# Long convolution and gated feed-forward on one core: some units of the third step taken out by ScalarE and GpSimd, and the first group's matrices made inside that step

## The chip, the cores and the metric

The kernel runs on one core of a Trainium2 chip. The metric is the device time of one execution in microseconds; the time of a kernel is the median over its runs. The engines are called PE (TensorE; its weight loads PEld), DVE (VectorE), ACT (ScalarE), POOL (GpSimd) and SP (SyncE, which here issues every DMA). Each takes its instructions in the order in which the program lists them.

## The reference

A batch of 4 sequences of 12480 positions and 128 channels goes through a gated convolution over the whole sequence, with a filter that a small network makes from position embeddings. The result goes, as 49920 rows, through a feed-forward layer of width 2048 whose gate is a cosine.

```
h_filt = (relu(pos_emb @ w1) @ w2) * exp(-0.01 * pos)[:, None]
Uf = rfft(x * v, n=2*S, axis=1);  Hf = rfft(h_filt, n=2*S, axis=0)
y  = irfft(Uf * Hf, n=2*S, axis=1)[:, :S, :]
t  = (x * y).reshape(B * S, D)
h  = t @ w_in
out = (h * cos(h)) @ w_out
```

Everything is float32; `w_in` and `w_out` come as 64-bit floats and are converted on the chip.

## The kernel before

The Fourier transforms are matrix products. A length is split as 96 x 120 (`N1`, `N2`), and a batch goes through four steps, all on one large buffer `slots` (128 partitions, 64 pairs of channels, 240 columns, 2): `f1` (units of one pair of channels, line 407 and its evictions), `f2` (units of two frequencies, a product with the filter's transform, lines 448 to 474), `i1` (the third step, 64 units of one pair of channels, lines 479 to 490) and `i2` (30 groups of four matrices each, lines 504 to 511), after which rows are ready for the feed-forward layer. Batch 0's first three steps stand alone at the start of the program; its `i2`, and all steps of the other three batches, are woven into the feed-forward layer's steps (lines 743 to 768), which fill PE for the rest of the time.

The order of work is written out by hand. Every piece of work is a Python generator, and what it emits between two yields lands in the engines' lists at that place. `units` runs the matmuls of unit j beside the evictions of unit j-1, and with `before(j)` prepares what unit j needs. `beside` runs one such generator, counts its yields i, and in between takes a step of `convert_units` (when i is a multiple of 14) or of a second generator (when i is a multiple of 5).

The third step of batch 0, in the stretch from about 270 to 337 us, is the call `beside(i1_units(bank), ..., some_groups)` at line 907. In it three kinds of work are mixed:

- `i1_units`: for each of 64 units PE makes four products into one of eight PSUM banks (the trace counts eight passes for them); ACT copies half of the bank to the tile `other` (line 487, two buffers); DVE takes the sum and the difference of the other half of the bank and `other` into `slots` (line 489, two instructions of 96 x 240).
- `convert_units`: eight pieces of `w_out`. For each, DVE takes exponent and mantissa (L133, L141), GpSimd makes the power (L135, L137), ACT converts two halves (L144, L146), GpSimd adds them (L147); one step later DVE joins the sign (L151) and GpSimd multiplies (L156). `raw` has three buffers, `low` one.
- `some_groups`: groups 2, 7, 12, 17, 22 and 27 of the matrices that `i2` needs. A matrix is two ACT instructions (L291, L296, the latter into `spare`, two buffers) and a GpSimd sum (L297); after four of them the group is stored to `td`. At its end, `next(backs[0])` makes group 0 in one go for the coming `i2` (tile `tm`: its first matrix with a GpSimd sum, the three others with L293 on DVE), and loads `xs`.

The tables `rows` and `tw_t` that the matrices are made from are loaded at line 899, once the second step's buffers are free. The second step's units end with two GpSimd sums each (L474), which write what `i1` reads. The first matmul of `i2` (L504) needs all of `slots` and group 0's matrices.

Of the kernel before, what the change touches and what calls it, by code (L numbers as in the profile page):

```python
# [9 lines left out]
F32 = mybir.dt.float32  # L10
# [20 lines left out]
def kernel(  # L31
# [46 lines left out]
    nc = tc.nc  # L78
# [4 lines left out]
    N1, N2 = 96, 120  # L83
# [16 lines left out]
    G = BANK // D  # L100
# [49 lines left out]
    def float32_join(dst, raw, power, high):  # L150
# [6 lines left out]
        if dst.space == DRAM:  # L157
# [5 lines left out]
                 for c in range(0, DFF, WCOL)]  # L163
    out_pieces = [(slice(c, c + WCOL // D), out_words[:, c:c + WCOL // D, :, :])
                  for c in range(0, NFC, WCOL // D)]
# [133 lines left out]
    def make_w(w, k1, **how):  # L299


        turn(w, even[:, 0, :], even[:, 1, :], tw_w[:, 0, k1:k1 + 1], tw_w[:, 1, k1:k1 + 1],
             **how)
# [149 lines left out]
            for r, src in enumerate((ftile[0:KE, :, k, :], above[0:KE, :, k - KF, :])):  # L453
                nc.tensor.matmul(pi[:, r], w[:, i, :], src, start=True, stop=True)

    def f2_product(pool, ps, h, k1, whole):


        y = parts[0:N2, :, k1:k1 + 2, :, :].rearrange("p r k b i -> p r b (k i)")
        t = pool.tile([N2, 2, CB, 4], F32, name="t", bufs=1 + whole)  # L460
        uu = ps[0:N2, :].rearrange("p (r b j) -> p r b j", r=2, j=4)
        if whole:
            for r, (dst, hh) in enumerate(((y, h[:, :, :, :]), (t[:, :, :, :], h[:, ::-1, :, :]))):
                u = uu[:, r]
                twice = bass.AP(tensor=u.tensor, offset=u.offset,
                                ap=[u.ap[0], [0, 2], *u.ap[1:]])
                nc.vector.tensor_tensor(dst, twice, hh, op=ALU.mult)  # L467
                yield
        for r, op in ((0, ALU.subtract), (1, ALU.add)):
            if not whole:  # L470
                nc.vector.tensor_tensor(y[:, r], uu[:, 0], h[:, r], op=ALU.mult)
                yield
                nc.vector.tensor_tensor(t[:, r], uu[:, 1], h[:, 1 - r], op=ALU.mult)
            nc.gpsimd.tensor_tensor(y[:, r], y[:, r], t[:, r], op=op)  # L474
            yield

    def i1_mm(ps, b, i):
# [3 lines left out]
                parts[0:N2, r, :, b, i],  # L481
                cs[:, r, :], start=True, stop=True)

    def i1_evict(pool, ps, b):
        pj = ps[0:N1, 0:4 * N2].rearrange("p (i r j) -> p r j i", i=2, r=2)
        other = pool.tile([N1, N2, 2], F32, name="other")
        nc.scalar.copy(out=other[:, :, :], in_=pj[:, 1])  # L487
        for h, op in ((0, ALU.add), (1, ALU.subtract)):
            nc.vector.tensor_tensor(slots[0:N1, b, h * N2:(h + 1) * N2, :], pj[:, 0],  # L489
                                    other[:, :, :], op=op)  # L490
            yield

    def i2_mm(ps, t, g, part):
# [36 lines left out]
    def units(n, steps, before, mm, after, parts, ahead=2, skip=0):  # L530


        for j in range(min(ahead, n)):
            for _ in before(j) or ():
                pass
        yield 0.0
        last = iter(())
        for j in range(n):
            early = iter(before(j + ahead) or () if j + ahead < n else ())
            now = None  # L540
            for i in range(parts):
                if i == skip or 2 * (i - skip) == max(parts, 2):
                    now = mm(j, now, int(i > skip))
                if i == 0 and parts == 1:
                    now = mm(j, now, 1)
                next(last, None)
                next(early, None)
                yield steps / parts
            for _ in early:
                pass  # L550
            next(last, None)
            last = after(j, now)
        for _ in last:
            pass
        yield REST

    SOME = range(2, NG, 5)
# [52 lines left out]
    def f2_both_units(bank):  # L610

        with tc.tile_pool(name="both", bufs=2) as pool:
            ws = {}

            def before(j):
                ws[j] = pool.tile([KE, 2, N2], F32, name="w")
                for i in range(2):
                    make_w(ws[j][:, i, :], 2 * j + i, half=bank)
                nc.sync.dma_start(wd[j, :, :, :], ws[j][:, :, :])

            def mm(j, ps, i):
                if i == 0:
                    ps = bank(), bank()
                for filt in range(2):
                    f2_mm(ps[filt], ws[j], 2 * j, i, filt=filt == 1)
                return ps

            def after(j, ps):
                h = pool.tile([N2, 2, CB, 4], F32, name="h", bufs=3)
                nc.scalar.activation(h[:, :, :, :].rearrange("p r b j -> p (r b j)"),  # L630
                                     ps[1][0:N2, :], AF.Copy, scale=1.0 / M)
                nc.sync.dma_start(hd[j, :, :, :, :], h[:, :, :, :])
                yield from f2_product(pool, ps[0], h, 2 * j, True)

            yield from units(N1 // 2, F2_STEPS, before, mm, after, 4, ahead=1)

    def i1_units(bank):
        with tc.tile_pool(name="mid", bufs=2) as pool:
            def mm(j, ps, i):
                if i == 0:  # L640
                    ps = bank()
                i1_mm(ps, j, i)
                return ps

            yield from units(CB, I1_STEPS, lambda j: None, mm,
                             lambda j, ps: i1_evict(pool, ps, j), 2)

    def make_group(pool, g, t, summed):

# [8 lines left out]

    def some_groups(pool):
        for g in SOME:  # L660
            t = pool.tile([N1, G, 2, R], F32, name="some", bufs=2)
            yield from make_group(pool, g, t, G)
        next(backs[0])

    def i2_units(bank, b, bufs):

        with tc.tile_pool(name="back", bufs=2, side="left" if b else "right") as pool:
            ts, xss = {}, {}

            def before(j):  # L670
                ts[j] = pool.tile([N1, G, 2, R], F32, name="tm", bufs=bufs)
                xss[j] = pool.tile([R, 2, UA * D], F32, name="xs", bufs=bufs)
                load_pairs(xss[j], x, b, n2s(j)[0], n2s(j)[UA])
                if b == 0 and j not in SOME:
                    return make_group(pool, j, ts[j], 1)
                nc.sync.dma_start(ts[j][:, :, :, :], td[j, :, :, :, :])

            def mm(j, ps, i):
                if i == 0:
                    ps = bank()  # L680
                i2_mm(ps, ts[j], j, i)
                return ps

            yield from units(NG, I2_STEPS, before, mm,
                             lambda j, ps: i2_out(pool, ps, xss.pop(j), b, j),
                             4 if b == 0 else 2, ahead=bufs - 1, skip=int(b == 0))

    def inverse_units(bank, b):

        if b + 1 == B:
            yield from i2_units(bank, b, 3)
            return
        new = u_units(b + 1, 3, slots[0:R, :, :, :],
                      lambda j, half: nc.gpsimd if b == 0 and j % 2 > half else nc.vector,
                      side="right" if b else "left")
        parts = 4 if b == 0 else 2
        for i, steps in enumerate(i2_units(bank, b, 2)):
            if i > 2 * parts:  # L700
                for _ in range(i % parts > 0 if b == 0 else 1 + i % 2):
                    next(new, None)
            yield steps * (FIRST_STEPS if b == 0 else I2U_STEPS) / I2_STEPS
        yield from new
# [95 lines left out]
    with tc.manual_schedule():  # L800
        with tc.tile_pool(name="psum", bufs=8, space=PSUM) as psum, \
                ExitStack() as first:
            def bank():
                return psum.tile([P, BANK], F32, name="ps")

            spool = ctx.enter_context(tc.tile_pool(name="slots", bufs=1))
            slots = spool.tile([P, CB, 2 * N2, 2], F32, name="slots")
# [64 lines left out]


            backs = [inverse_units(lambda: bank(), b) for b in range(B)]

            def beside(units, pieces, more=lambda pool: iter(())):
                with tc.tile_pool(name="convert", bufs=1) as pool:
                    convert, other = convert_units(pool, pieces), more(pool)
                    for i, _ in enumerate(units):
                        if i % 14 == 0:  # L880
                            next(convert, None)
                        elif i % 5 == 0:
                            next(other, None)
                    for _ in [*convert, *other]:
                        pass
# [17 lines left out]
            w_out_sb = wpool.tile([P, NFC, D], F32, name="w_out_sb")  # L903
            quarter = wpool.tile([P, 1], F32, name="quarter")
            nc.vector.memset(quarter[:, :], 0.25)
            nc.sync.dma_start(w_in_sb[:, :], wind[:, :])
            beside(i1_units(bank), [(w_out_sb[:, c, :], w) for c, w in out_pieces], some_groups)

        ps_acc = ctx.enter_context(tc.tile_pool(name="ps_acc", bufs=1, space=PSUM))
        ps_h = ctx.enter_context(tc.tile_pool(name="ps_h", bufs=4, space=PSUM))  # L910
# [36 lines left out]
        steps = [(n, c) for n in range(NALL) for c in range(NFC)]  # L947
        hidden, gates, ots, obs = {}, {}, {}, {}
        for i in range(len(steps) + LAG):
            if i < len(steps):  # L950
                n, c = steps[i]
# [53 lines left out]
```

## Time and profile before

| | |
|---|---|
| median of four runs | 3759.27 us |
| lowest and highest run | 3757.18, 3764.23 us |
| the profiled execution | 3757.18 us, span 3755.4 us |
| PE, DVE, ACT, POOL busy over the span | 98%, 74%, 67%, 68% |
| granted PE clock, mean | 0.996 |
| second step of batch 0 | about 168 to 271 us |
| third step of batch 0 | 271.07 (first i1 pass) to 336.62 (first i2 pass) |

The page's first part gives the busy time of each engine, the windows view the same for a stretch of time. A timeline shows one instruction, or a run of like ones (`x8`), per line: start, length, engine, line of the program, operation, result and operands with their shapes, and in brackets how long the engine had stood idle and which instruction let it go. A length is that of the instruction, not the distance to the next start, which is shorter on DVE and ACT, where successive instructions overlap.

### The profile page before, as it was taken

What the parts mean: (1) busy time and instruction counts of PE and PEld (TensorE: products, weight loads), DVE (VectorE), ACT (ScalarE), POOL (GpSimd) and SP (SyncE); (2) the same over time, 40 slices, a digit from 0 to 9 for tenths busy, and PEclk for the clock granted to TensorE, in tenths of its full rate; (3) what the DMA queues carried; (4) which work ended last, traced back from release to release, by engine and by line L of the source; (5) the groups of instructions that cost most, each with busy time, mean ns of one, the idle gap of its engine ahead of it and who ended that gap; (6) DMA issues with size and microseconds to landing.
All of it is one profiled execution on the core that took longest, in us unless ns stands there. A gap on an engine that the chain in (4) does not pass through costs nothing.

```text
span 3755.4 us, 47177 instructions
## 1 busy us (share of the span) xinstructions
PE 3687.4 (98%) x13546; PEld 2106.4 (56%) x13546; DVE 2772.9 (74%) x5586; ACT 2508.3 (67%) x4660; POOL 2558.6 (68%) x2318
## 2 busy tenths in 40 slices
PE   7898999999999999999999999999999999999999
PEld 6777555555566556555565556555566544444444
DVE  8887997777866787788767776788765566666666
ACT  5756777766655557766655567666664677777777
POOL 7666775588845665688745664788644677777776
PEclk9999999999999999999999999999999999999999
DMA  6263551022203550122104530122105200000000
GB/s 167 66 184 109 155 165 36 24 76 75 72 13 94 178 151 12 42 78 79 50 18 130 181 102 21 52 80 76 37 21 175 73 23 17 17 23 18 17 23 13
DMA packets 209499, 276.14 MB, mean 74 GB/s; under 512 B 17111, under 2 KB 146535, under 8 KB 209111
## 3 DMA queue, kind: packets, MB, share of 16 engines
q1 hardware_dynamic: 209239, 273.12, 24.3%
q8 instruction: 109, 1.79, 0.2%
q14 instruction: 151, 1.24, 0.1%
HBM read 193.64 MB, written 79.42 MB: 73 GB/s over the span
## 4 chain that ended last, share of the span: by engine, by line
PE 88%; DVE 3%; DMA 3%; POOL 2%; ACT 2%; issue 1%; SPq 0%; POOLq 0%; ACTq 0%; DVEq 0%
PE ph L743 34%; PE acc L768 29%; PE cv L504 5%; PE cv L768 5%; PE cv L479 4%; PE cv L448 3%; PE cv L407 3%; PE ph L126 2%; DMA hd<-h 2%; PE ps L407 2%; POOL f L752 1%; DMA tm<-td 1%; DVE slots L489 1%; ACT cs L757 0%; DVE k L749 0%
## 5 line engine op out<-in xcount | busy, mean ns | idle before, releaser
L752 POOL TENSOR_TENSOR f<-a,k 128x512 f32<-128x512 f32 (+1 forms) x1568 | 1985.6, 1266 | 1058.8 <-DVE k L749 1057.4
L743 PE MATMUL ph<-at,w_in_sb 128*128 128x512 f32 (+1 forms) x3136 | 1598.1, 591 | 3.5 <-DVE gt L759 2.6
L746 ACT ACTIVATE a<-ph,quarter 128x512 f32<-128x512 f32 (+1 forms) x1568 | 1071.2, 683 | 701.1 <-PE ph L743 692.0
L768 PE MATMUL acc<-gt,w_out_sb 128*128 128x512 f32 (+1 forms) x2688 | 1369.4, 591 | 0.0
L759 DVE TENSOR_TENSOR gt<-ph,cs 128x512 f32<-128x512 f32 (+1 forms) x1568 | 1077.6, 687 | 359.1 <-ACT cs L757 341.6
L757 ACT ACTIVATE cs<-f 128x512 f32<-128x512 f32 (+1 forms) x1568 | 981.0, 626 | 368.7 <-POOL f L752 366.6
L749 DVE TENSOR_SCALAR k<-a 128x512 f32<-128x512 f32 (+1 forms) x1568 | 794.8, 507 | 548.8 <-ACT a L746 523.3
L768 PEld LDWEIGHTS acc<-gt,w_out_sb 128*128 128x128 f32 x2688 | 508.0, 189 | 642.4 <-issue 631.4
L743 PEld LDWEIGHTS ph<-at,w_in_sb 128*128 128x128 f32 x3136 | 552.9, 190 | 337.6 <-issue 257.4
L474 POOL TENSOR_TENSOR slots<-slots,t 120x256 f32<-120x256 f32 x384 | 312.8, 820 | 60.0 <-DVE t L467 25.6
L504 PEld LDWEIGHTS cv<-slots,tm 96*104 96x104 f32 x1920 | 238.8, 169 | 105.8 <-issue 88.8
L504 PE MATMUL cv<-slots,tm 96*104 96x128 f32 x1920 | 251.5, 273 | 9.6 <-POOL tm L297 5.0
L768 PE MATMUL cv<-gt,w_out_sb 128*128 128x512 f32 (+1 forms) x448 | 224.5, 583 | 1.1 <-DVE gt L759 1.1
L479 PEld LDWEIGHTS cv<-cs,slots 120*96 120x96 f32 x1536 | 176.6, 167 | 67.2 <-issue 65.2
L479 PE MATMUL cv<-cs,slots 120*96 120x120 f32 x1536 | 183.2, 266 | 0.0
L448 PEld LDWEIGHTS cv<-slots,w 124*120 124x120 f32 x576 | 103.7, 184 | 124.3 <-issue 112.4
L407 PEld LDWEIGHTS cv<-c,slots 104*124 104x124 f32 x768 | 132.5, 192 | 72.4 <-issue 59.4
L448 PE MATMUL cv<-slots,w 124*120 124x256 f32 x576 | 173.0, 380 | 0.0
L407 PE MATMUL cv<-c,slots 104*124 104x192 f32 x768 | 151.7, 327 | 5.9 <-DVE gt L759 3.5
L768 PEld LDWEIGHTS cv<-gt,w_out_sb 128*128 128x128 f32 x448 | 84.9, 190 | 104.8 <-issue 99.5
L489 DVE TENSOR_TENSOR slots<-cv,other 96x240 f32<-96x240 f32 x384 | 133.2, 394 | 1.5 <-ACT other L487 1.4
L395 DVE TENSOR_TENSOR xt<-xt,vt 104x256 f32<-104x256 f32 x177 | 133.0, 753 | 0.0
(131 smaller groups left out, 2514.1 us busy)
## 6 DMA issues: line engine op xcount, KB each, us to landing
h<-hd SPq DMA_DIRECT2D x144, 240.0 KB
tm<-td SPq DMA_DIRECT2D x96, 312.0 KB
xt<-in_x_dram SPq DMA_DIRECT2D x120, 208.0 KB
vt<-in_v_dram SPq DMA_DIRECT2D x120, 208.0 KB
xs<-in_x_dram SPq DMA_DIRECT2D x120, 208.0 KB
zd<-zs SPq DMA_DIRECT2D x119, 208.0 KB
zb<-zd SPq DMA_DIRECT2D x96, 256.0 KB
w<-wd SPq DMA_DIRECT2D x144, 116.2 KB
```

The lines of the kernel that those rows point to most:

```text
L407: nc.tensor.matmul(ps[0:KE, i * 2 * N1:(i + 1) * 2 * N1], u[:, b, 0:KE, i], c1[0:u.shape[0], :, :].rearrange("p r k -> p (r k)"), start=Tr ...
L448: nc.tensor.matmul(pi, w[:, i, :], parts[0:KE, :, k], start=True, stop=True)
L474: nc.gpsimd.tensor_tensor(y[:, r], y[:, r], t[:, r], op=op)
L479: nc.tensor.matmul(ps[0:N1, (i * 2 + r) * N2:(i * 2 + r + 1) * N2], parts[0:N2, r, :, b, i], cs[:, r, :], start=True, stop=True)
L504: nc.tensor.matmul(ps[0:R, i * D:(i + 1) * D], t[:, i, r, :], slots[0:N1, :, place, :], start=(r == 0), stop=(r == 1))
L743: nc.tensor.matmul(ph[:, 0:m], w_in_sb[:, c * P:(c + 1) * P], ats[n][:, 0:m], start=True, stop=True)
L746: nc.scalar.activation(a[:, 0:m], ph[:, 0:m], AF.Identity, bias=quarter[:, 0:1], scale=INV_TWO_PI)
L749: nc.vector.tensor_scalar(out=k[:, 0:m], in0=a[:, 0:m], scalar1=ROUND, scalar2=ROUND, op0=ALU.add, op1=ALU.subtract)
L752: nc.gpsimd.tensor_tensor(f[:, 0:m], a[:, 0:m], k[:, 0:m], op=ALU.subtract)
L757: nc.scalar.activation(cs[:, 0:m], f[:, 0:m], AF.Sin, scale=TWO_PI)
L759: nc.vector.tensor_tensor(gt[:, 0:m], ph[:, 0:m], cs[:, 0:m], op=ALU.mult)
L768: nc.tensor.matmul(accs[n][:, 0:m], w_out_sb[:, c, :], gt[:, 0:m], start=(c == 0), stop=(c == NFC - 1))
```

## The change

Five edits go together.

- `i1_evict` can take a unit out in another way: ACT also copies the first half of the bank, to a tile `base`, and GpSimd takes the sum and the difference from `base` and `other`. In the third step of batch 0 this is done for units 1, 7, 13, ... 61 (11 of 64), and `other` has four buffers there instead of two. The other batches' `i1` is as before.
- `units` yields after each piece of `before` at its start, where it ran them through in one go. So group 0 comes in five pieces; `some_groups` takes them ahead of group 27, with a yield after each, and `inverse_units` passes the four new yields on.
- `beside` takes a step of the conversion when i is a multiple of 13, and one of the second generator when i divided by 9 leaves 1 or 5: 27 steps instead of 24. The second generator has 29 now, so that two matrices of group 27 come behind the last unit, where group 0's four came before.
- The same 13 holds for the first step of batch 0, beside which `w_in` is converted (it has no second generator).
- The last unit of the second step of batch 0 has its two sums on DVE instead of GpSimd.

The lists of the engines then differ so: in the third step ACT has 11 copies more, DVE 22 sums fewer and GpSimd 22 more. Behind GpSimd's sums for unit 61 there stand three of the 24 L297 sums of the groups. ACT's first pair of matrix instructions stands ahead of its first `other`.

```diff
-    def f2_product(pool, ps, h, k1, whole):
+    def f2_product(pool, ps, h, k1, whole, sums=nc.gpsimd):
...
-            nc.gpsimd.tensor_tensor(y[:, r], y[:, r], t[:, r], op=op)
+            sums.tensor_tensor(y[:, r], y[:, r], t[:, r], op=op)
...
-    def i1_evict(pool, ps, b):
+    def i1_evict(pool, ps, b, gpsimd=False, bufs=2):
         pj = ps[0:N1, 0:4 * N2].rearrange("p (i r j) -> p r j i", i=2, r=2)
-        other = pool.tile([N1, N2, 2], F32, name="other")
+        other = pool.tile([N1, N2, 2], F32, name="other", bufs=bufs)
         nc.scalar.copy(out=other[:, :, :], in_=pj[:, 1])
+        first, engine = pj[:, 0], nc.vector
+        if gpsimd:
+            base = pool.tile([N1, N2, 2], F32, name="base")
+            nc.scalar.copy(out=base[:, :, :], in_=first)
+            first, engine = base[:, :, :], nc.gpsimd
         for h, op in ((0, ALU.add), (1, ALU.subtract)):
-            nc.vector.tensor_tensor(slots[0:N1, b, h * N2:(h + 1) * N2, :], pj[:, 0],
-                                    other[:, :, :], op=op)
+            engine.tensor_tensor(slots[0:N1, b, h * N2:(h + 1) * N2, :], first,
+                                 other[:, :, :], op=op)
             yield
...
         for j in range(min(ahead, n)):
             for _ in before(j) or ():
-                pass
+                yield 0.0
...
-                yield from f2_product(pool, ps[0], h, 2 * j, True)
+                yield from f2_product(pool, ps[0], h, 2 * j, True,
+                                      nc.vector if 2 * j + 2 == N1 else nc.gpsimd)
...
-                             lambda j, ps: i1_evict(pool, ps, j), 2)
+                             lambda j, ps: i1_evict(
+                                 pool, ps, j, shared and j % shared == 1,
+                                 4 if shared else 2), 2)
...
         for g in SOME:
+            if g == SOME[-1]:
+                for _ in range(G + 1):
+                    next(backs[0])
+                    yield
             t = pool.tile([N1, G, 2, R], F32, name="some", bufs=2)
             yield from make_group(pool, g, t, G)
-        next(backs[0])
...
-        for i, steps in enumerate(i2_units(bank, b, 2)):
+        back = i2_units(bank, b, 2)
+        for _ in range(0 if b else G):
+            yield next(back)
+        for i, steps in enumerate(back):
...
-                        if i % 14 == 0:
+                        if i % 13 == 0:
                             next(convert, None)
-                        elif i % 5 == 0:
+                        elif i % 9 in (1, 5):
                             next(other, None)
...
-            beside(i1_units(bank), [(w_out_sb[:, c, :], w) for c, w in out_pieces], some_groups)
+            beside(i1_units(bank, 6), [(w_out_sb[:, c, :], w) for c, w in out_pieces], some_groups)
```

## The prediction

> **What bounds the kernel now.** I read the windows view by stages first, then inside the one stage that the change touches the instruction timelines of PE, GpSimd (POOL) and DVE, then the waits.
>
> ```profile
> core 0: us, PE busy (x) PEld busy (x) DVE busy (x) ACT busy (x) POOL busy (x), PEclk, DMA share, GB/s
> 168.00:270.00 102.00, 95.88 (x480) 74.55 (x480) 85.69 (x192) 55.59 (x148) 66.26 (x94) 0.98 0.59 172
> 270.00:338.00 68.00, 57.40 (x518) 55.96 (x519) 51.19 (x157) 44.62 (x137) 46.86 (x63) 0.94 0.27 84
> 338.00:420.00 82.00, 80.31 (x348) 49.69 (x346) 70.42 (x130) 58.52 (x122) 58.12 (x57) 0.98 0.54 166
> ```
>
> The third step of batch 0 is the row 270 to 338. Before it and behind it PE is busy; the 3400 us behind it are bound by PE (98% of the span), so what this stage gains or loses is passed on whole. In the stage no engine is full: DVE 51 of 68, GpSimd 47, ACT 45.
>
> ```profile
> 271.75 30.40 PE L479 MATMUL ps<-cs,slots 120*96 120x120 f32 x278 [0.23 <-POOL slots L474]
> 303.42 5.96 PE L479 MATMUL ps<-cs,slots 120*96 120x120 f32 x56 [1.27 <-DVE slots L489]
> ...
> 330.56 1.04 PE L479 MATMUL ps<-cs,slots 120*96 120x120 f32 x8 [0.82 <-DVE slots L489]
> 336.62 4.78 PE L504 MATMUL cv<-slots,tm 96*104 96x128 f32 x24 [5.02 <-POOL tm L297]
> ```
>
> PE's timeline shows the turn: 278 passes without a hole, until the eight banks are full, then bursts of 56 passes (seven units of eight) that wait for evictions on DVE. PE ends i1 at 331.6 and waits five us for the last sums and for group 0. So from 302 on the evictions set the pace: 64 units from 273.23 to 336.08, 0.98 us each, though DVE needs 0.72 (two L489).
>
> ```profile
> 286.62 0.85 POOL L156 TENSOR_TENSOR w_out_sb<-sig,power 128x256 f32<-128x256 f32 x1 [0.77 <-DVE power L151]
> 287.44 1.07 POOL L135 TENSOR_SCALAR power<-power 128x256 uint32<-128x256 uint32 x1
> 288.59 1.07 POOL L137 TENSOR_SCALAR power<-power 128x256 uint32<-128x256 uint32 x1
> 289.75 0.73 POOL L147 TENSOR_TENSOR sig<-sig,low 128x256 f32<-128x256 f32 x1
> 290.43 1.21 POOL L297 TENSOR_TENSOR some<-some,spare 96x208 f32<-96x208 f32 x2
> 292.15 0.62 POOL L297 TENSOR_TENSOR some<-some,spare 96x208 f32<-96x208 f32 x1 [0.51 <-ACT spare L296]
> 293.54 0.85 POOL L156 TENSOR_TENSOR w_out_sb<-sig,power 128x256 f32<-128x256 f32 x1 [0.77 <-DVE power L151]
> ```
>
> One conversion period on GpSimd, 6.9 us for seven units. Starts, not durations, give its prices: L156 0.82, L135 1.15, L137 1.16, L147 0.68, so a piece costs 3.81; a sum L297 costs 0.605. The idle figure on L156 is GpSimd waiting for DVE's L151.
>
> ```profile
> 299.58 0.41 DVE L151 SCALAR_TENSOR_TENSOR power<-raw,power 128x256 uint32<-128x256 uint32 x1
> 299.91 1.40 DVE L133 TENSOR_SCALAR power<-raw 128x256 uint32<-128x256 uint32 x1
> 301.23 0.28 DVE L141 TENSOR_SCALAR sig<-raw 128x256 uint32<-128x256 uint32 x1
> 302.55 3.24 DVE L489 TENSOR_TENSOR slots<-ps,other 96x240 f32<-96x240 f32 x10 [1.04 <-ACT other L487]
> ```
>
> DVE at the fourth piece. After L141 it stands 1.04 us, because ACT has its own two conversion steps (L144, L146) ahead of the next `other`: this hole, eight times, is most of DVE's lost time. And L133 took 1.40 where its siblings take 0.28: GpSimd was then in a sum (299.67) and in L156 (from 300.44 to 301.16) back to back.
>
> **The change part by part.**
>
> *Eleven units to ACT and GpSimd.* Units 1, 7, ... 61 leave DVE: 22 L489 at 0.328 (ten in 3.24) = 7.2 us off DVE. ACT gains 11 copies `base`; two `other` start 0.25 apart (0.59 for two), so 2.8 us on 45 of 68: room. GpSimd gains 22 sums of 96x240, which the trace lacks. Below, a sum of 96x208 costs 0.605; above, L156 of 128x256 costs 0.82, and the 128x256 add L147, which is nearest in form, 0.68. I take 0.67, since 240 columns stand two thirds of the way from the first to the last: 14.7 us (13.3 to 18.0).
>
> Can GpSimd hold it? In before its stage runs from the first sum at 275.92 (which waits for ACT's first `spare`, and that for the tables' load; not moved) to the end of `tm` at 336.57, 60.6 us. Work in it: 8 pieces x 3.81 = 30.5, 24 sums x 0.605 = 14.5, `tm` 0.6, together 45.6; idle 15.0. The new work is as large as all of that idle. Up to unit 61's second sum (the order has three of the 24 sums behind it) GpSimd must now do 30.5 + 21 x 0.605 + 0.6 + 14.7 = 58.5. From 275.92, never idle, that ends at 334.4; the step behind may not start before, since its first matmul reads all of `slots`.
>
> It will not be never idle. Each L156 needs L151, and L151 stands in DVE's queue behind sums whose `other` ACT copies; ACT in turn can be at most four units ahead, and the buffers of the GpSimd units come free only when GpSimd has gone through the conversion ahead of them. So the pause at each piece stays: of the eight L156, four show 0.77, two 1.40, and those at 300.44 and 335.27 none, as a late sum filled it. I take 0.77 x 8 = 6.2 (bounds 0 and 8 x 1.40 = 11.2), and the 1.25 ahead of the first L135, which waits for DVE and not for GpSimd's own work. 334.4 + 6.2 + 1.2 = 341.8.
>
> *Holds on DVE.* Where GpSimd has a backlog when DVE comes to L151 or L133, DVE waits as at 299.91: 1.1 us. Once in eight pieces before; with GpSimd full I take one more on the path (bounds 0 and 8 x 1.1 = 8.8): 342.9.
>
> The Trainium skill has a rule that speaks against the change: "SBUF — State Buffer", section "Who interferes with whom", says that a DVE instruction with two SBUF inputs, or in a two-port mode, and a GpSimd instruction that reads SBUF shut each other out for a whole instruction, by order of issue. The row at 299.91 agrees in kind (1.40 against 0.28). By the rule alone all eight L151 and L133 pairs would meet a GpSimd instruction and wait for what is left of it, and the evictions, with one input in PSUM, would not; by the row the wait went on through two GpSimd instructions. The first would make the sum some 3 us longer by my estimate (eight halves of 0.7), the second up to 8.8.
>
> *Four `other` buffers instead of two.* ACT may run ahead, but not past L144, which waits for DVE's L141; the hole of 1.04 stays. In my sum they only keep ACT from waiting on every GpSimd unit: nothing gained, and without them the wait for GpSimd would come after two units instead of four.
>
> *Group 0 made inside the step.* Its 5 ACT, 1 GpSimd and 3 DVE instructions leave the end. On the path they cost little: the last L489 ended at 336.08, `tm` let PE go at 336.62: 0.5 us, already in the comparison of ends. Behind it, two pairs of group 27 now come last: ACT 4 x 0.37 = 1.5, GpSimd 1.2; hidden by PE's first 16 passes at 0.199 (4.78 / 24) = 3.2 us, ahead of which group 1 is not needed. If that cover went, 1 us. The earlier `xs` load and `td` store on SP's queue stand ahead of the store of group 27, which is read much later: nothing.
>
> *Tables a step earlier, conversion each 13 steps.* ACT's first pair now stands ahead of the first `other`, and waits for the tables (275.02) where `other` started at 272.84; PE has eight banks (64 passes) to fill meanwhile: nothing. Conversions ending at step 117 instead of 126 raise GpSimd's share per step, and are in its sum. In the first step of batch 0 the same 13 moves the conversions of `w_in`; there ACT is full to the end (168.75) with the same list of work: nothing, with 0.4 either way for another hole.
>
> *Last sums of the second step on DVE.* `t` ends at 270.16; two DVE sums of 120x256 (nearest: L401 and L395 of 104x256, 0.41 at the least, 0.76 at the median beside GpSimd) end at 270.6 and 271.0 instead of 270.98 and 271.70. PE starts 0.4 earlier, but GpSimd's start hangs on the tables: nothing (at most 0.7 gained).
>
> *Sum.* The next step starts at 342.9 + 0.3 for the last two units on DVE = 343.2 against 336.62: +6.6. PE's wait ahead of it stays over three us, as long as the hole from 268.0 to 271.07 behind which the window from 270 to 276 shows a granted clock of 0.72, so the slow first passes stay. On this execution's 3757.2 (span 3755.4 and 1.8 around it) that is 3763.8; it lies 2.1 below the median of the four, so **3766** for the median.
>
> **The rivals.**
>
> *A, GpSimd keeps up (faster).* If the backlog fills every pause, the step ends with GpSimd's bare work at 334.4, and PE, no longer five us idle, keeps its clock: 16 passes at 0.111 (eight L504 in 0.89 in later pieces of the chain of waits) instead of 0.199 save 1.4. 336.62 - 334.5 + 1.4 = -3.5: 3755.8. For it: 15.0 idle against 14.7 new. Against it: the pauses are a ring through DVE and ACT, not spare time. It decides where the pauses and holds fall under 3.5 us in all (336.62 - 334.5 + 1.4). More than 7 us of gain is excluded by the 58.5 of bare work.
>
> *B, more collisions (much slower).* Sums at L156's 0.82 (+3.3) and the hold of 1.1 at all eight pieces (+7.7): up to +17.6; halfway, +12: 3771. For it: 299.91; against: it came once in eight.
>
> *C, no change.* The ring of DVE, ACT and GpSimd around each conversion keeps its 6.9 us per seven units, whoever evicts: within 2 us, 3757 to 3761. Against it: a period of 13 steps holds 3.81 + 2.7 x 0.605 + 2.2 x 0.67 = 6.9 of GpSimd work for 6.5 units, with no pause in it.
>
> **How the numbers follow.** About 0.2%, 7.5 us, is what a measurement of this kernel can tell from no change. Forecast (+3 to +10) 0.46, B 0.32, A 0.12, C 0.10. Of the forecast two fifths lie above 7.5, with B: slower 0.50. Of A half is given to faster, for scatter between runs: 0.06. The rest, 0.44, is same. Range: 3756 (A's time) to 3775 (B short of its top), about 0.2 left out; the forecast's own is 3762 to 3769.
>
> **What would show it.** In the stage GpSimd busy about 60 of 70, with back-to-back sums and idle only ahead of L156 and the first L135; L133 or L151 over 1 us two to five times; ACT waiting for GpSimd's sums ahead of `other`; PE's first L504 pass between 340 and 346. A start under 336 makes the forecast wrong (A), over 347 is B. GpSimd sums of 96x240 starting more than 0.8 apart would make my price wrong.

## The result, and the profile after

| | before | after |
|---|---|---|
| median of all runs | 3759.39 us (53 runs) | 3766.2 us (33 runs) |
| ratio to before, 95% interval | 1 | 1.0019 (1.0014 to 1.0023) |
| profiled execution, span | 3757.18, 3755.4 | 3770.36, 3768.2 |
| last `f2` pass (line 454) | 267.63 | 268.16 |
| first pass of `i2` | 336.62 | 344.06 |
| between the two | 68.99 | 75.90 |

The change makes the kernel 6.8 us slower by the medians. The profiled execution of after lies 4 us above its median, that of before 2 us below its own, so the two spans differ by more than that. Two starts in the trace show where the time went without most of this scatter: from the last `f2` pass (line 454) to the first `i2` pass (L504 before, L509 after) the step takes 6.9 us longer, which is the loss of the medians. What follows it took 3418.8 us in before and 3424.1 in after; in the twelve other kernels below, which have the same work there, it took 3418.8 to 3422.9, whatever was edited in the step.

In after, lines beyond 474 have moved: the evictions are L494 (DVE's and GpSimd's alike), the copy of `base` is L491, `i2` starts at L509.

The windows view by stages (columns as named in its head):

```profile
core 0: us, PE busy (x) PEld busy (x) DVE busy (x) ACT busy (x) POOL busy (x), PEclk, DMA share, GB/s
270.00:344.00 74.00, 56.62 (x512) 53.51 (x512) 49.69 (x138) 44.17 (x143) 60.03 (x82) 1.00 0.26 81
344.00:426.00 82.00, 80.31 (x350) 50.71 (x351) 69.58 (x128) 59.34 (x125) 58.92 (x58) 0.98 0.54 164
```

GpSimd is busy 60.0 of 74 us where it was busy 46.9 of 68; DVE shows only 1.5 us less, though 7.2 were taken from its list; 3.9 of the difference are instructions of DVE that ran longer than usual beside GpSimd (they are called held, and told of below). No engine is full. PE's timeline:

```profile
271.25 16.91 PE L479 MATMUL ps<-cs,slots 120*96 120x120 f32 x160 [2.70 <-POOL slots L474]
289.46 4.32 PE L479 MATMUL ps<-cs,slots 120*96 120x120 f32 x40 [1.30 <-DVE slots L494]
...
335.70 4.32 PE L479 MATMUL ps<-cs,slots 120*96 120x120 f32 x40 [0.66 <-ACT tm L291]
344.06 4.52 PE L509 MATMUL cv<-slots,tm 96*104 96x128 f32 x24 [4.04 <-DVE slots L494]
```

PE first stops after 160 passes, where before ran 278 without a hole. That alone is no sign of the loss. ACT's first pair of matrix instructions, which waits for the tables, now stands ahead of its first `other`, so that this starts at 276.15 instead of 272.84; e1 (below), which has the same late start and no moved units, stops even earlier and loses nothing:

```profile
271.38 11.88 PE L479 MATMUL ps<-cs,slots 120*96 120x120 f32 x112 [2.71 <-POOL slots L474]
```

Where DVE's time goes is in the waits view, before and then after (us in total, times, longest us):

```profile
DVE slots L489 <- ACT other L487: 14.6, 24, 1.4
```

```profile
DVE slots L494 <- ACT other L487: 23.6, 25, 4.4
ACT sig L144 <- DVE sig L141: 14.9, 8, 3.0
ACT other L487 <- POOL slots L494: 9.5, 7, 2.0
```

DVE's longest wait, 4.4, is that late start; e1 has one of 4.8 in a total of 15.6. The last line is new. ACT stands 9.5 us because the next `other` needs a buffer that a GpSimd unit still holds, and DVE then stands for ACT. How this closes into a ring is to be read in the chain of waits of after (start, length, what the chain goes through), one turn of it:

```profile
306.76 0.73 POOL sig L147
307.49 1.32 POOL slots L494 x2
308.81 0.02 issue
308.83 0.36 ACT other L487
309.19 0.02 issue
309.22 0.30 DVE slots L494
...
309.54 1.02 DVE slots L494 x3
310.56 0.65 DVE power L151
311.21 1.39 DVE power L133
312.61 0.08 issue
312.68 1.08 POOL power L135
...
313.84 0.75 POOL power L137
...
314.99 0.73 POOL sig L147
315.72 0.66 POOL slots L494
316.38 0.02 issue
316.41 0.05 ACT other L487
```

From one L147 to the next is 8.23 us for six or seven units. GpSimd's conversion and its sums for a unit free a buffer; ACT fills it; DVE does two units and its part of the next piece; and only then can GpSimd go on. The groups' sums (L297) are not on the chain here; GpSimd's timeline shows that they lie beside ACT's and DVE's part of the turn:

```profile
308.76 1.20 POOL L297 TENSOR_TENSOR some<-some,spare 96x208 f32<-96x208 f32 x2
310.24 0.69 POOL L297 TENSOR_TENSOR some<-some,spare 96x208 f32<-96x208 f32 x1 [0.28 <-ACT spare L296]
310.89 0.87 POOL L494 TENSOR_TENSOR slots<-base,other 96x240 f32<-96x240 f32 x1
311.72 0.72 POOL L156 TENSOR_TENSOR w_out_sb<-sig,power 128x256 f32<-128x256 f32 x1
```

Not every turn is as long. Here are the first, fifth and last of the eight L156 in after:

```profile
287.29 0.85 POOL L156 TENSOR_TENSOR w_out_sb<-sig,power 128x256 f32<-128x256 f32 x1 [0.43 <-DVE power L151]
...
320.61 0.77 POOL L156 TENSOR_TENSOR w_out_sb<-sig,power 128x256 f32<-128x256 f32 x1
...
340.16 0.73 POOL L156 TENSOR_TENSOR w_out_sb<-sig,power 128x256 f32<-128x256 f32 x1 [1.30 <-DVE power L151]
```

The first four turns take 33.3 us and the last three 19.6. In e1, with no unit moved, the same turns take 25.9 and 19.1. So the loss lies in the first four turns, and four of ACT's seven waits for a GpSimd unit, 6.7 of the 9.5 us, fall into them. But GpSimd is nearly full there too: the four pieces, 12 groups' sums and 10 sums of units in them are 29.1 us of work by their prices. Which of the two holds the turn, the trace alone doesn't tell.

### The profile page after: what moved, and what is told of

It is laid out like the page before. It is cut to its first block, busy times and chain, and to the rows that moved or that the text cites. A ratio compares the mean times of both kernels' runs of the same rounds, so it can differ in the third digit from the quotient of the medians.

```text
span 3768.2 us, 47191 instructions
## 1 busy us (share of the span) xinstructions
PE 3693.0 (98%) x13546; PEld 2106.8 (56%) x13546; DVE 2764.2 (73%) x5566; ACT 2512.4 (67%) x4671; POOL 2574.2 (68%) x2338
## 4 chain that ended last, share of the span: by engine, by line
PE 85%; POOL 2%; DVE 2%; DMA 1%; ACT 1%; issue 1%; SPq 0%; POOLq 0%; DVEq 0%; ACTq 0%
PE ph L758 33%; PE acc L783 28%; PE cv L509 5%; PE cv L783 5%; PE cv L479 4%; PE cv L407 3%; PE cv L448 3%; PE ph L126 2%; POOL f L767 1%; DMA tm<-td 1%; ACT cs L772 0%; DVE k L764 0%; DVE gt L774 0%; POOL slots L474 0%; DVE slots L494 0%
## 5 line engine op out<-in xcount | busy, mean ns | idle before, releaser
L509 PEld LDWEIGHTS cv<-slots,tm 96*104 96x104 f32 x1920 | 238.4, 169 | 108.6 <-issue 94.0
L509 PE MATMUL cv<-slots,tm 96*104 96x128 f32 x1920 | 251.5, 273 | 11.7 <-DMA tm<-td 7.7
L494 DVE TENSOR_TENSOR slots<-cv,other 96x240 f32<-96x240 f32 x384 | 133.1, 394 | 1.5 <-ACT other L487 1.4
```

The costliest lines, as they stand in the source:

```text
L509: nc.tensor.matmul(ps[0:R, i * D:(i + 1) * D], t[:, i, r, :], slots[0:N1, :, place, :], start=(r == 0), stop=(r == 1))
```

## The experiments

All stand in one table. "Step" is the time from the last `f2` pass to the first `i2` pass in the one profiled execution of each kernel; differences of it under about 1 us are not built upon. Ratios are to before, over several rounds, with the 95% interval.

| kernel | ratio (interval) | first `i2` pass | step | against before |
|---|---|---|---|---|
| before | 1 | 336.62 | 68.99 | 0 |
| after | 1.0019 (1.0014, 1.0023) | 344.06 | 75.90 | +6.9 |
| e1 no units moved | 1.0003 (0.9994, 1.0012) | 337.46 | 69.16 | +0.2 |
| e2 units moved alone | 1.0019 (1.0010, 1.0028) | 345.00 | 76.09 | +7.1 |
| e3 two buffers | 1.0047 (1.0034, 1.0060) | 352.74 | 85.61 | +16.6 |
| e4 every twelfth unit | 1.0005 (0.9996, 1.0014) | 339.29 | 71.73 | +2.7 |
| e5 after, no group sums | 1.0011 (1.0002, 1.0020) | 341.84 | 73.79 | +4.8 |
| e6 before, no group sums | 1.0001 (0.9992, 1.0010) | 336.26 | 68.07 | -0.9 |
| e7 before, late halves | 0.9989 (0.9981, 0.9998) | 332.93 | 64.58 | -4.4 |
| e8 late halves, no units moved | 0.9976 (0.9968, 0.9985) | 332.03 | 62.55 | -6.4 |
| e9 own buffers | 1.0009 (1.0000, 1.0018) | 340.55 | 72.48 | +3.5 |
| e10 own buffers, no group sums | 0.9996 (0.9987, 1.0005) | 334.73 | 67.47 | -1.5 |
| e11 own buffers, late halves | 1.0006 (0.9997, 1.0015) | 339.59 | 70.36 | +1.4 |
| e12 as e11, no group sums | 0.9977 (0.9967, 0.9986) | 328.62 | 60.72 | -8.3 |

**Which edit costs.** e1 is after without the moved units; e2 is before with the moved units and their four buffers, and nothing else of the change.

```diff
-            beside(i1_units(bank, 6), [(w_out_sb[:, c, :], w) for c, w in out_pieces], some_groups)
+            beside(i1_units(bank), [(w_out_sb[:, c, :], w) for c, w in out_pieces], some_groups)
```

> The changed kernel with all 64 units of the third step left to DVE (two buffers for `other`, as before); group 0 inside the step, the 13 and the sums on DVE stay. Theory (GpSimd is full with the 22 added sums): the first i2 pass comes at 335 to 338 us, where before has 336.6, and the time is 3757 to 3761. Rival (the other edits cost the time: tables ahead of the first `other`, conversions closer together, group 0): the pass stays near 344 and the time near 3766.

```diff
-            beside(i1_units(bank), [(w_out_sb[:, c, :], w) for c, w in out_pieces], some_groups)
+            beside(i1_units(bank, 6), [(w_out_sb[:, c, :], w) for c, w in out_pieces], some_groups)
```

> The kernel before with nothing but the eleven units moved to ACT and GpSimd and four buffers for `other`. Theory: all of the loss is here, first i2 pass at 342 to 346 us, time 3764 to 3767. Rival (other edits): 335 to 338 us, time 3757 to 3761.

e1 gives the step of before (+0.2), e2 that of after (+7.1), and the ratios agree. All of the loss comes with the moved units; group 0 inside the step, the tables' place, the 13 steps and the last sums of the second step come out at nothing together.

**How much the four buffers do.** e3 is after with two `other` buffers.

```diff
-                                 4 if shared else 2), 2)
+                                 2), 2)
```

> The changed kernel with two buffers for `other` instead of four. Theory (ACT waits for buffers that GpSimd frees late, behind a conversion): ACT then waits after two units instead of four, the first i2 pass moves from 344 to 350 to 355 us, time 3772 to 3777. Rival (the buffers do nothing, the loss is collisions of DVE with GpSimd alone): 344 us and 3766.

The step is 9.7 us longer than in after. The same waits as above, in e3 (us in total, times, longest us):

```profile
DVE slots L494 <- ACT other L487: 32.6, 28, 4.4
PE ps L479 <- DVE slots L494: 15.1, 10, 2.4
...
ACT other L487 <- POOL slots L494: 13.3, 7, 3.3
```

ACT's wait for GpSimd units grows from 9.5 to 13.3 us (the longest from 2.0 to 3.3), DVE's for `other` from 23.6 to 32.6, and PE's for DVE from 9.1 to 15.1. GpSimd's list of work is the same as in after, so a full GpSimd alone would not explain the 9.7 us: the wait for buffers is part of what sets the pace.

**Half the units.** e4 moves units 1, 13, ... 61, six of 64.

```diff
-            beside(i1_units(bank, 6), [(w_out_sb[:, c, :], w) for c, w in out_pieces], some_groups)
+            beside(i1_units(bank, 12), [(w_out_sb[:, c, :], w) for c, w in out_pieces], some_groups)
```

> The changed kernel with every twelfth unit moved instead of every sixth: six units, 12 sums on GpSimd instead of 22. Theory: 10 sums of 0.67 are 6.7 us less work on GpSimd, of which pauses give back some: first i2 pass at 338 to 341 us, time 3760 to 3763. Rival (a fixed cost of the new way, or of the other edits): 343 to 344 us, 3765 to 3766.

+2.7 against +6.9, as expected: six units cost 0.46 us each and the next five 0.83 each. Of the two numbers of units that were tried, neither pays; for six the interval of the ratio does not exclude no change.

**GpSimd's list, or the ring?** e5 takes 24 sums, 14.5 us by the price of 0.605, off GpSimd in after; e6 does the same in before. The matrices of these groups then lack one half, so the two kernels, and e10 and e12 below, only serve to read times.

```diff
-            nc.gpsimd.tensor_tensor(dst, term, spare, op=ALU.add)
+            if add:
+                nc.gpsimd.tensor_tensor(dst, term, spare, op=ALU.add)
...
-                make_t(t[:, i, :, :], n2, spare=spare[:, :, :])
+                make_t(t[:, i, :, :], n2, spare=spare[:, :, :], add=summed < G)
```

> The changed kernel without the 24 GpSimd sums (L297) of the six groups made beside the third step; ACT still writes both halves of each matrix, so the matrices stored for these groups lack one half. 14.5 us less work on GpSimd, nothing less on ACT, DVE and PE. Theory (GpSimd is full): the step shortens by 6 us or more, first i2 pass at 333 to 338 us, time 3754 to 3760. Rival (the ring of DVE and ACT around the conversions sets the pace, and GpSimd's work lies in its shade): under 2 us, 342 to 344 us, time about 3765.

> The kernel before without the same 24 sums (the stored matrices lack one half). Theory (in before GpSimd has 15 us of idle time and does not set the pace): at most 2 us, first i2 pass at 334 to 337 us, time 3756 to 3760. Rival (GpSimd set the pace in before too): as much as in the changed kernel, 328 to 331 us, time about 3752.

In e6 the first `i2` pass came as expected: before does not hang on GpSimd's list. e5 failed its expectation. With the bare work down from 58.5 to some 46 us, the first `i2` pass came at 341.84 instead of between 333 and 338; the step is only 2.1 us shorter than in after, nearly what the rival had (under 2). GpSimd's timeline in e5 shows where the freed time went:

```profile
294.50 0.85 POOL L156 TENSOR_TENSOR w_out_sb<-sig,power 128x256 f32<-128x256 f32 x1 [2.27 <-DVE power L151]
...
298.32 1.35 POOL L495 TENSOR_TENSOR slots<-base,other 96x240 f32<-96x240 f32 x2
302.25 0.85 POOL L156 TENSOR_TENSOR w_out_sb<-sig,power 128x256 f32<-128x256 f32 x1 [2.58 <-DVE power L151]
```

The pause ahead of these two L156, 0.46 and 0.77 in after, is 2.3 and 2.6: the turn is still 7.75 us (294.50 to 302.25), against 8.32 in after, now with an idle GpSimd in it. In later turns GpSimd stands ahead of the sums instead, for ACT's `base`. The first four turns together take 31.2 us instead of 33.3, which is the 2.1 us; the last three take 19.8, as good as in after. The theory of the prediction, that GpSimd's list sets the step, falls here, and a second one takes its place: two limits lie close together, the list and the ring of buffers, and removing either alone leaves the other. e9 to e12 put it to the test.

**ACT's half of a conversion moved later.** The hole of 1.04 us on DVE behind each L141 was in before too. In e7, on before, ACT's two conversions and GpSimd's sum of the halves are put five steps later, so that the next `other` does not stand behind L144 and L146.

```diff
+        return power, sig
+
+    def float32_sum(pool, raw, power, sig):
         high = sig[:, :].bitcast(F32)
...
                 half = float32_parts(pool, raws[i])
+                yield
+                half = float32_sum(pool, raws[i], *half)
...
-                        if i % 14 == 0:
+                        if i % 14 == 0 or i % 14 == 5 and i > 5:
                             next(convert, None)
-                        elif i % 5 == 0:
+                        if i % 14 and i % 5 == 0:
                             next(other, None)
```

> The kernel before with the second half of each conversion (ACT's L144 and L146, GpSimd's L147) written out five steps of the loop later than DVE's L141 instead of right behind it. Theory (before loses its time in the hole of 1.04 us that DVE has at each of eight pieces, since ACT's two steps wait for DVE's L141 and stand ahead of the next `other`): the holes go, first i2 pass at 328 to 331 us, time 3751 to 3754. Rival (DVE's own work or GpSimd sets the pace): under 2 us, time 3757 to 3760.

The step is 4.4 us shorter, less than was expected (the first `i2` pass came at 332.93 and not by 331), but clearly so. DVE's timeline in e7 (its L154 is before's L151):

```profile
305.70 0.41 DVE L154 SCALAR_TENSOR_TENSOR power<-raw,power 128x256 uint32<-128x256 uint32 x1
306.03 0.28 DVE L133 TENSOR_SCALAR power<-raw 128x256 uint32<-128x256 uint32 x1
306.24 0.28 DVE L141 TENSOR_SCALAR sig<-raw 128x256 uint32<-128x256 uint32 x1
306.44 1.97 DVE L494 TENSOR_TENSOR slots<-ps,other 96x240 f32<-96x240 f32 x6
```

The evictions go on behind L141 without a hole. DVE's wait for `other` is 7.9 us where it was 14.6: about half of what DVE waited in before went with this hole, without any of its work going to another engine. Shorter holes have come in other places (0.86 ahead of the sums at 309.26).

e8 puts the same late halves into after, with group 0 inside the step, no unit moved and three `other` buffers.

```diff
-                                 pool, ps, j, shared and j % shared == 1,
-                                 4 if shared else 2), 2)
+                                 pool, ps, j, shared and j % shared == 64,
+                                 3 if shared else 2), 2)
...
-                        if i % 13 == 0:
+                        if i % 14 == 0 or i % 14 == 5 and i > 5:
                             next(convert, None)
-                        elif i % 9 in (1, 5):
+                        if i % 14 and i % 9 in (3, 7):
                             next(other, None)
```

> The changed kernel with no units moved (three buffers for `other`), conversions every 14 steps with their second half five steps later, and a matrix where the step divided by 9 leaves 3 or 7; group 0 in pieces and the last sums of the second step on DVE stay. Theory: as e7, first i2 pass at 328 to 331 us, time 3750 to 3754, and PE waits less than in before ahead of i2 for group 0. Rival (group 0's pieces or the tables cost something by themselves): 333 us or later.

This version beats both kernels: 3752.75 us, ratio 0.9976 (0.9968 to 0.9985) to before, though its `i2` starts a microsecond later than expected. Its step is 2.0 us shorter than e7's, so the other edits of the change, worth nothing in e1, seem to be worth something once the hole is gone; which of them, no run separates. Its stage in the windows view:

```profile
core 0: us, PE busy (x) PEld busy (x) DVE busy (x) ACT busy (x) POOL busy (x), PEclk, DMA share, GB/s
270.00:332.00 62.00, 53.83 (x512) 52.83 (x512) 54.67 (x161) 43.87 (x133) 47.47 (x61) 0.98 0.34 103
```

DVE is busy 54.7 of 62 with all 64 units on its list, against 51.2 of 68 in before.

**Both limits taken apart.** In e9 the GpSimd units have `other` buffers of their own, and `base` has three, so that no unit of DVE waits for a buffer that GpSimd holds. e10 is e9 without the 24 sums, e11 is e9 with the late halves, e12 is both.

```diff
-        other = pool.tile([N1, N2, 2], F32, name="other", bufs=bufs)
+        other = pool.tile([N1, N2, 2], F32, name="other_g" if gpsimd else "other",
+                          bufs=3 if gpsimd else bufs)
...
-            base = pool.tile([N1, N2, 2], F32, name="base")
+            base = pool.tile([N1, N2, 2], F32, name="base", bufs=3)
```

> The changed kernel, in which the units taken out by GpSimd have `other` and `base` tiles of their own (three each), so that no unit of DVE waits for a buffer that GpSimd holds. Theory now (two limits lie close together in the step: the ring through buffers and conversions, and GpSimd's list of work with the pauses and holds at each conversion): freeing one gives little, first i2 pass 2 to 3 us earlier, at 341 to 342.5 us, time 3763 to 3765. Rival (the shared buffers alone carry the loss): 336 to 339 us, 3758 to 3761.

> As the run with own buffers, and without the 24 sums L297 of the six groups (the matrices stored for these groups lack one half). Theory of two limits: with the buffers free, taking 14.5 us of work off GpSimd counts for more than the 2 us that it gave alone; first i2 pass at 335 to 338 us, 5 us before the run with the sums; time 3757 to 3761. Rival (GpSimd's work does not matter at all): within 2.5 us of the run with the sums.

> The run with own buffers, and with the second half of each conversion (L144, L146, L147) five steps of the loop later, as in the run that made before faster. Theory of two limits: the ring is gone, but GpSimd's list of 58.5 us is still there; first i2 pass at 340 to 342.5 us, time 3762 to 3765, no better than own buffers alone. Rival (the ring was all): 331 to 335 us, time 3754 to 3757.

> As the run with own buffers and late halves, and without the 24 sums L297 (the matrices stored for these groups lack one half). Theory of two limits: both are off; first i2 pass at 329 to 333 us, some 10 us before the same kernel with the sums; time 3751 to 3756. Rival (collisions between DVE and GpSimd, which stay, set the pace): 337 us or later.

In the first `i2` pass e9 came 0.5 us earlier than its range, e10 and e12 just before theirs (0.3 and 0.4), e11 0.4 before its own; the medians lie in theirs. What the 24 sums are worth, each time against the kernel that differs in nothing else, answers the question:

| in which kernel | step with the sums | without | difference |
|---|---|---|---|
| before | 68.99 | 68.07 | -0.9 |
| after | 75.90 | 73.79 | -2.1 |
| own buffers | 72.48 | 67.47 | -5.0 |
| own buffers and late halves | 70.36 | 60.72 | -9.6 |

The same 14.5 us of GpSimd work are worth little while the ring is closed and 9.6 us once it is open. Conversely, opening the ring with both repairs gives 5.5 us with the sums in place (75.90 to 70.36) and 13.1 without them (73.79 to 60.72). From its first L135 (281.80) to the start of `i2`, GpSimd has no pause left in e11; a part of its timeline:

```profile
317.64 0.69 POOL L500 TENSOR_TENSOR slots<-base,other_g 96x240 f32<-96x240 f32 x1
318.30 0.72 POOL L159 TENSOR_TENSOR w_out_sb<-sig,power 128x256 f32<-128x256 f32 x1
318.99 1.07 POOL L135 TENSOR_SCALAR power<-power 128x256 uint32<-128x256 uint32 x1
320.14 1.08 POOL L137 TENSOR_SCALAR power<-power 128x256 uint32<-128x256 uint32 x1
```

There the list alone is the limit, as the prediction had it for after: it takes 61.5 us (277.55 to 339.1) for the 58.5 of bare work, and `i2` starts at 339.59. ACT still waits for GpSimd in e9 and e11, now for `spare`, which the groups' sums free late (5.3 and 10.2 us). Leaving out the sums removes this wait together with the work, so the 5.0 of e9 need not all be work; in e11, where GpSimd never stands, it costs nothing of its own. In e12 neither binds, and PE's timeline shows a third limit, PE's own work:

```profile
270.98 55.73 PE L485 MATMUL ps<-cs,slots 120*96 120x120 f32 x512 [2.70 <-POOL slots L480]
328.62 3.17 PE L516 MATMUL cv<-slots,tm 96*104 96x128 f32 x24 [1.91 <-DVE slots L501]
```

512 passes run without a hole. But e12 leaves work out. With all of it done, e11, which has the moved units and both repairs, has 70.36, and e8, without moved units, 62.55; the two differ in the order of work and the number of buffers too (14 steps against 13), so the 7.8 us are not the price of the moved units alone.

## Why the prediction was right in time and half right in cause

- **Units off DVE and onto ACT.** Right as a count. DVE gained nothing by it: it waits 23.6 us for `other` instead of 14.6 (15.6 in e1).
- **The price of a GpSimd sum.** Predicted 0.67. Two of them start at 284.17 in after and the next instruction at 285.48: 0.655 each. Rival B's 0.82 is out.
- **GpSimd's list.** Predicted 58.5 bare from the first sum to the second sum of unit 61, and 8.5 of pauses and holds around it (6.2, 1.25 and 1.1). In after it ran from 276.33 to 342.75, 66.4 us, so 7.9 around the 58.5. Of that the pauses ahead of L156 were 3.5 (0.43, 0.46, 0.77, 0.50, 1.30, and three of none), ahead of L135 1.15, and 2.1 were waits ahead of groups' sums, which the prediction did not have; the rest, 1.2, is sums that ran longer and short gaps. The total was right by terms that made up for each other.
- **The step that failed** is the one that turned this list into the end of the step: "So the pause at each piece stays", with every pause and all the bare work added up on one path. The prediction had seen the ring and then priced it as a pause of GpSimd only. The chain of after shows a turn of 8.2 us made of all three engines, with the groups' sums beside it, and e5 showed that some 12.7 us less of the bare 58.5 shorten the step by 2.1. The number came out by luck: the two limits lie within a few microseconds of each other, so a sum for one of them gave nearly the time of both.
- **The four buffers: "nothing gained".** Mis-sized. Without them the step is 9.7 us longer (e3); and separate ones take another 3.4 off (e9). The prediction named the mechanism and set no price to it.
- **Holds on DVE.** Predicted one more of 1.1. Summing what L151, L133 and L141 took beyond 0.41, 0.28 and 0.28, before had 1.1 us in one instruction and after 5.0 in eight, at four of the eight pieces. The forecast's sign to look for, L133 or L151 over 1 us two to five times, came twice (L133 with 1.46 and 1.43; L141 once with 1.36). The two of L133 lie on the chain; the first, shown above, delays L135 and what hangs on it. Holds alone don't make the loss: e10 and e12 have 3.7 and 4.5 us of them and shorter steps than before. How much of the 5.0 us is lost in the end stays open; a kernel with the moved units and without holds was not tried.
- **The hole of 1.04.** Right that it stays (313.84 in after). Not said was that it could be removed, which is worth 4.4 us in before (e7).
- **Group 0, tables, 13 steps, last sums: nothing.** Right for all of them together (e1).
- **The next step's start.** 343.2 predicted, 344.06 found; +6.6 against +6.9 in the step and +6.8 in the medians. GpSimd's list ended within 0.2 us of the predicted 342.9, but what follows it took 1.3 us instead of 0.3: ACT copied the last `other` only after GpSimd's last sum (342.81), and DVE's last two sums began at 343.20.
- **Rivals.** A needed pauses and holds under 3.5 us; they were 7.9. C held that the ring keeps its pace whoever evicts: the ring is there, but the moved units lengthen it, and the interval of e2 leaves no change out. B's start over 347 did not come; its holds came at four of the eight pieces, without its price for the sums.

## What to carry to other kernels

An engine's idle time is spare only if it is not a link of a ring: before moving work to it, follow which buffer the moved work holds, who refills that buffer, and what stands ahead of its release in the new engine's list. When a measured time agrees with a sum, the cause is not yet shown; take a suspected limit away alone, then together with the other one, since with two limits close by each alone looks worthless. And where an engine waits right behind a small step in another's list, try first to move that step a few places later: here this gained 4.4 us, where giving the waiting engine's work away lost 6.9.

## What the hardware showed beyond that

**Holds reach further than one instruction.** L133 in after began at 311.14 and took 1.46 against 0.28. On GpSimd a sum ran from 310.89 to 311.76 and L156 from 311.72 to 312.44, so DVE waited through the rest of one and all of the other. The Trainium skill ("SBUF — State Buffer", section "Who interferes with whom") says, of a DVE instruction in a two-port mode, that whoever issues first has the shared pair of ports for the whole instruction and the other is blocked. The block agrees, but here one that stood in wait did not get its turn between two instructions of GpSimd. L141 is held as well, right behind an L133 that was not (DVE's timeline in after):

```profile
318.40 0.90 DVE L151 SCALAR_TENSOR_TENSOR power<-raw,power 128x256 uint32<-128x256 uint32 x1
319.23 0.28 DVE L133 TENSOR_SCALAR power<-raw 128x256 uint32<-128x256 uint32 x1
319.43 1.36 DVE L141 TENSOR_SCALAR sig<-raw 128x256 uint32<-128x256 uint32 x1
```

The sum of holds is 1.1 us in before, 5.0 in after and 10.7 in e11, where GpSimd never pauses. How full GpSimd is does not order them alone: before and e5 have 44.6 and 45.3 us of GpSimd work from 276 us to the start of `i2`, and 1.1 and 4.1 us of holds.

**The same hole of PE, different clocks.** Ahead of the first i1 pass PE stood 2.70 us in after and in e12 alike. In the window from 271 to 274 us the granted clock was 1.00 in after and 0.50 in e12. Of the ten kernels with this hole seven show 1.00 there, and e3, e11 and e12 0.64, 0.68 and 0.50. After 1.91 us (e12, ahead of `i2`) the 24 passes took 3.17 us, after 4.04 (after) 4.52. The Trainium skill ("TensorE: Matmul & The Clock Gate", Part 1) says that PE's clock falls to half after at least one idle window of about 3.4 us, and that the window is free-running. By that a hole of 2.70 us should not have cost any clock, and in three of the ten it did; where the windows lay, no trace here shows. In e12, where PE is the limit, it counts: the 20 passes that began before 275 us took 4.29 us, while after had 35 passes in 3.98.
